# One matmul per tile for rows and gate logits, and one accumulation for places and counts, in a fused attention and expert kernel

## The chip, the cores and the metric

The kernel runs on one core of one Trainium2 chip. The time is the device time of one execution in microseconds (us). Before the change it is 1401.14 us, the median of 3 runs (1400.79 to 1401.62). The profile shown below is of one further execution, with a span of 1395.5 us. A core has five engines that run side by side, each with an instruction queue in order of its own: TensorE (PE, with its weight loads listed apart as PEld), VectorE (DVE), ScalarE (ACT), GpSimd (POOL) and SyncE (SP, which only issues transfers here). TensorE writes to PSUM; in this kernel ScalarE copies nearly all of it from there to SBUF.

## The reference

Two stages follow each other. The first is attention that keeps, for each query, only the 32 largest of its 576 scores:

```python
B, H, S, D = 8, 8, 576, 64
scores = q @ k.T / sqrt(D)                       # per batch and head
kth    = np.partition(scores, -32)[..., -32]     # the 32nd largest of each row
attn   = softmax(where(scores >= kth, scores, -1e9))
out    = attn @ v                                # (B, H, S, D)
```

The outputs of the heads are put side by side as rows of x, 4608 rows (tokens) of 512 numbers. The second stage sends each row through one of eight experts:

```python
logits = x @ w_gate                              # (4608, 512) @ (512, 8)
expert = argmax(logits); gate = softmax(logits)[expert]
y      = relu(x @ w1[expert]) @ w2[expert]       # 512 -> 1024 -> 512
out    = gate * y                                # in the order of the tokens
```

All numbers are 32-bit floats.

## The kernel before

**Units and groups.** Two heads make a unit, so a batch has four units (`n.u` is 0 to 3) and the kernel has 8 batches of four. The 576 queries of two heads are nine tiles of 128 rows. Two tiles make a group, so two units make nine groups and a batch has 18; the kernel has 144 groups. Each group goes through: scores on TensorE (line 269), copied to SBUF by ScalarE (line 276); the search for the 32nd largest on VectorE (lines 283 to 338); the mask and the exponential on ScalarE and GpSimd (lines 363, 372, 380); the transposes of the weights on TensorE (lines 391, 402, 404), copied by ScalarE (lines 395 to 412).

**The end of a unit.** When all tiles of a unit are done, `outputs` multiplies the transposed weights with the values (lines 424, 425) and ScalarE copies the result to `oT`, which holds the unit's outputs with the features on the partitions (128 partitions, two heads of 64) and the queries along the row. Then, tile by tile (KC = 5 tiles, the last a half):

- TensorE turns `oT` round by five transposes (lines 432 and 434), four into the PSUM bank `px` and one into the bank `pl`. These are rows of x.
- TensorE multiplies the same five tiles of `oT` with the gate's weights of this unit, `wg2`, 16 columns wide (8 experts for each of two heads; the other head's rows are zero) (line 437), also into `pl`.
- ScalarE copies the logits to `lt` (line 443), four tiles of rows to `x` (line 444) and the fifth (line 445).
- GpSimd divides both by the softmax sums: `logits` (lines 459 to 464) multiplies `lt` by the reciprocals `rz` and adds up `lg`, `rows` (line 470) multiplies the rows in place in `x`.

**The end of a batch.** `choice` (VectorE) finds each token's expert as a one-hot matrix `oh`. `ranks` (TensorE, lines 501 to 507) gives each token its place among the rows of its expert: how many tokens stand before it in its tile (a product with the triangle `before`), plus the tokens of the tiles ahead (products with `ones`), plus the running counts `run` (a product with the identity). A second chain in the same bank sums the new counts. `places` (VectorE, from line 517) reads the places, ScalarE copies the new counts to `run` (line 846), GpSimd scatters the rows to the experts' regions in HBM (line 538), and `table` (VectorE) lists the blocks of 128 rows that are full.

**The experts.** A full block is fetched, turned (line 655), multiplied with `w1` (line 680) and `w2` (line 695), scaled and scattered to the output (line 701). The products are cut into pieces, which are laid between the attention work of later batches.

**What sets the order.** The order of TensorE, ScalarE and VectorE is that of the program text, written by hand. `loop` walks over the 144 groups. A unit's end is a generator, `ending`, that goes on at named places in the groups after the unit's last: "products" (behind the scores of a later group), "relu" (on ScalarE ahead of the next copies of scores, line 276), "small", "rows" and so on. How many pieces of expert work go into which group is computed when the program is built, from a credit; it doesn't depend on the time that anything takes. Hence also fixed: what is left over for the end. All PSUM banks of the attention, `px`, `pl` and `rank` among them, are handed out in turn from a pool of two (`ps_t`, tag "t").

## Time and profile before

| stretch of the trace, us | what runs | busy share |
|---|---|---|
| 0 to 396 | attention of batches 0 to 2, almost no expert work | DVE 98%, PE 75% |
| 396 to 1112 | attention of batches 3 to 7 with expert work between | DVE 99%, PE 98% |
| 1112 to 1136 | last unit, last batch's choice and ranks | PE 91% |
| 1136 to 1380 | remaining expert blocks, 14.45 us each | PE 100%, DVE 2% |

The share of busy time over the whole run (PE 91%, DVE 79%) mixes these stages and says little; each is to be read by itself. The timeline lists every instruction with its start, its duration and the idle time of its engine ahead of it. Line 283 is the first VectorE instruction of each group's search, so the distance from one start of line 283 to the next is the time of a group. The sum over 18 groups gives the time of a batch:

| batch | 0 | 1 | 2 | 3 | 4 | 5 | 6 | 7 (17 groups) |
|---|---|---|---|---|---|---|---|---|
| time, us | 124.6 | 131.0 | 132.2 | 135.5 | 139.2 | 148.5 | 140.6 | 141.4 |
| PE busy in it, us | 91.2 | 98.9 | 104.8 | 133.1 | 136.3 | 146.8 | 137.9 | 139.7 |

In the first batches a plain group takes 7.02 us, with VectorE busy in all of it. From batch 3 on groups of 7.02 us stand beside groups of 8 to 9.7 us.

### The profile page before, as it was taken

How to read it: one execution, taken by the hardware profiler on the slowest of the kernel's cores; microseconds unless marked ns; L12 is line 12 of the kernel's file. 1: busy time of each engine (PE TensorE's matmuls, PEld its weight loads, DVE VectorE, ACT ScalarE, POOL GpSimd, SP SyncE). 2: the span in 40 equal slices, each digit the busy share in tenths (PEclk: the TensorE clock that was granted, in tenths of full speed). 3: DMA queues.
4: the chain of work that ended last, by engine and by line, in shares of the span. 5: the costliest groups of instructions: out<-in, count | busy, mean ns of one | idle time of the engine just before them, and what ended most of it. 6: DMA issues, size and time to landing. Idle time of an engine off the chain costs nothing. (4 is left out here: it accounts for less than half of the span.)

```text
span 1395.5 us, 24818 instructions
## 1 busy us (share of the span) xinstructions
PE 1267.8 (91%) x7778; PEld 872.2 (62%) x7778; DVE 1106.4 (79%) x4653; ACT 920.6 (66%) x2081; POOL 650.0 (47%) x804
## 2 busy tenths in 40 slices
PE   5777787677899999999999999999999999999995
PEld 3444454444567676767676666767676667677773
DVE  7999999999999999999999999999999920000000
ACT  4788878787888888787877787787777821111110
POOL 3455547455655665466555655565556521000000
PEclk8788878888899999999999999999999999999998
DMA  2000011001674266417553573357541859999890
GB/s 81 28 28 28 28 36 55 28 29 43 208 268 139 69 253 244 152 62 260 200 195 138 184 262 132 112 178 289 182 168 56 320 174 345 377 309 332 306 325 19
DMA packets 102222, 231.70 MB, mean 166 GB/s; under 512 B 5182, under 2 KB 25918, under 8 KB 102080
## 3 DMA queue, kind: packets, MB, share of 16 engines
q1 hardware_dynamic: 95328, 209.76, 42.9%
q0 software_dynamic: 6464, 19.97, 3.9%
q8 instruction: 63, 1.03, 0.3%
q14 instruction: 79, 0.65, 0.1%
q10 hardware_dynamic: 288, 0.30, 0.1%
HBM read 208.72 MB, written 22.33 MB: 166 GB/s over the span
## 5 line engine op out<-in xcount | busy, mean ns | idle before, releaser
L372 POOL TENSOR_TENSOR w<-s,w 128x576 f32<-128x576 f32 x288 | 407.6, 1435 | 464.0 <-ACT w L363 464.0
L680 PE MATMUL ph<-xTs,w 128*128 128x128 f32 x2560 | 311.7, 278 | 6.0 <-ACT xTs L657 6.0
L680 PEld LDWEIGHTS ph<-xTs,w 128*128 128x128 f32 x2560 | 301.4, 194 | 23.2 <-issue 14.9
L695 PE MATMUL py<-w,hT 128*128 128x512 f32 x640 | 292.9, 597 | 0.8 <-ACT hT L685 0.8
L331 DVE MAX8 tops<-scr 128x8 f32<-128x168 f32 x864 | 250.0, 323 | 0.1
L269 PE MATMUL sc<-qkb 64*128 64x288 f32 (+1 forms) x1280 | 224.0, 476 | 9.7 <-ACT s L276 5.2
L380 ACT ACTIVATE w<-w,nbias 128x576 f32<-128x576 f32 x288 | 224.7, 798 | 2.9 <-POOL w L372 2.8
L363 ACT ACTIVATE w<-s,low 128x576 f32<-128x576 f32 x288 | 207.6, 768 | 4.7
L391 PE MATMUL wTm<-ident,w 128*128 128x128 f32 x1152 | 173.7, 289 | 27.2 <-ACT x L444 17.8
L994 DVE CAST any_i<-pd 1x1 int32<-1x1 f32 x1 | 0.1, 146 | 237.6 <-PE pd L992 237.6
L695 PEld LDWEIGHTS py<-w,hT 128*128 128x128 f32 x640 | 114.5, 190 | 118.0 <-issue 115.6
L391 PEld LDWEIGHTS wTm<-ident,w 128*128 128x128 f32 x1152 | 139.1, 148 | 75.6 <-ACT x L444 19.0
L338 DVE MATCH_REPLACE8 scr<-tops,scr 128x168 f32<-128x168 f32 x576 | 178.9, 317 | 0.0
L276 ACT COPY s<-sc 128x576 f32<-128x576 f32 x288 | 170.5, 648 | 11.2 <-PE sc L269 11.1
L397 ACT COPY wT<-wTm 128x512 f32<-128x512 f32 x256 | 140.3, 609 | 41.4 <-PE wTm L391 41.2
L269 PEld LDWEIGHTS sc<-qkb 64*128 64x128 f32 (+1 forms) x1280 | 119.7, 198 | 74.1 <-issue 27.0
L424 PE MATMUL po<-wT,vb 128*64 128x288 f32 x1024 | 153.8, 448 | 0.4 <-ACT wTt L412 0.4
L701 POOL DMA_INDIRECT out_dram<-y,xg x40 | 41.7, 1043 | 216.4 <-ACT y L709 210.9
L322 DVE MAX8 few<-l 128x8 f32<-128x288 f32 x288 | 129.1, 448 | 0.0
L283 DVE TENSOR_TENSOR h<-s 128x576 f32<-128x576 f32 x144 | 115.9, 805 | 7.9 <-ACT s L276 7.9
L685 ACT ACTIVATE hT<-ph 128x512 f32<-128x512 f32 x80 | 48.9, 612 | 110.2 <-PE ph L680 110.2
L424 PEld LDWEIGHTS po<-wT,vb 128*64 128x64 f32 x1024 | 74.0, 150 | 76.2 <-issue 27.2
(127 smaller groups left out, 1524.4 us busy)
## 6 DMA issues: line engine op xcount, KB each, us to landing
w<-in_moe_w_dram SPq DMA_DIRECT2D x80, 2048.0 KB, 9.7
qkb<-in_qk_dram SPq DMA_DIRECT2D x31, 608.0 KB, 4.6
xg<-x_rows SPq DMA_DIRECT2D x40, 257.0 KB, 9.9
vb<-in_v_dram SPq DMA_DIRECT2D x32, 320.0 KB, 3.2
x_rows<-blank SPq DMA_DIRECT2D x5, 257.0 KB, 16.0
x_rows<-blank POOLq DMA_DIRECT2D x4, 257.0 KB, 9.0
x_rows<-x,posi POOLq DMA_INDIRECT x40, 3.1
out_dram<-y,xg POOLq DMA_INDIRECT x40, 6.2
```

The costliest lines, as they stand in the source:

```text
L269: nc.tensor.matmul(ps[rows, j, 0:HF], n.q[d, cols], n.k[d, keys], start=True, stop=True)
L276: lambda m=m, ps=ps: nc.scalar.copy(s[:, m, :, :], ps[:, :, 0:HF]) for m, ps in enumerate(got)
L331: nc.vector.max(out=tops[:, m, r * 8:(r + 1) * 8], in_=src[m])
L338: nc.vector.match_replace(out=scr[:, m, :], in_to_replace=tops[:, m, r * 8:(r + 1) * 8], in_values=src[m], imm_value=NEG,)
L363: nc.scalar.activation(w[:, m, :], s[:, m, :, :].rearrange("p j k -> p (j k)"), AF.Relu, scale=-STEEP, bias=low[:, m:m + 1],)
L372: k.last_pool = in_turn(nc.gpsimd.tensor_tensor(w[:, m, :], s[:, m, :, :].rearrange("p j k -> p (j k)"), w[:, m, :], op=ALU.subtract)).ins
L380: nc.scalar.activation(w[:, m, :], w[:, m, :], AF.Exp, scale=scale, bias=nbias[:, m:m + 1], accum_out=n.z[:, c:c + 1])
L391: nc.tensor.transpose(pm[:, c * P:(c + 1) * P], w[:, m, first:first + P], ident)
L397: nc.scalar.copy(wT[:, :, m, q], pm4)
L424: nc.tensor.matmul(po[r, 0:HF], n.v[:, c, r], wT[:, c, h, q], start=(c == 0), stop=False)
L680: nc.tensor.matmul(ph[:, f, :], n.w1[:, 0, dt, fc * P:(fc + 1) * P], n.xT[:, dt, :], start=(dt == 0), stop=(dt == DT - 1),)
L695: nc.tensor.matmul(py, hT[:, f, :], n.w2[:, 0, f, :], start=(f == 0), stop=(f == FT - 1))
```

## The change

For each tile of a unit's `oT`, the rows and the logits now come from one matmul: `oT` is loaded as the weights once, and the moving operand is a row of the new constant `turn`, in which the identity (128 columns) and the gate's weights of the unit (16 columns) stand side by side. The product is 144 columns wide. The five transposes and the separate gate products go away. Three tiles go to a first bank (432 columns), two to a second (288 columns), and ScalarE copies each bank with one instruction to a new tile `xl` in SBUF (one buffer), in place of the three copies to `lt` and `x`. GpSimd's instructions keep their number and shapes; `logits` reads and writes within `xl`, and `rows` now reads `xl` and writes `x`. For odd and even units the 16 columns stand on different sides of the identity, so that `turn` needs one identity for two units.

In `ranks`, the counts become a sixth tile of the places: one accumulation, 48 columns wide, started by the identity with `run` repeated six times. The second chain of products goes away.

The rest saves memory for that: the integer tiles of `iota_f` share one buffer, `slot_max` shrinks to two numbers that are repeated on reading, and two tiles of `table` get one buffer.

```diff
+    lw = 2 * E
+    turn = const.tile([P, U // 2, P + 2 * lw], F32, name="turn")
+    nc.vector.memset(turn, 0.0)
+    ident = turn[:, 0, lw:lw + P]
     make_identity(nc, ident)
+    for two in range(1, U // 2):
+        nc.gpsimd.tensor_copy(turn[:, two, lw:lw + P], ident)
...
-    for h in range(2):
-        r = slice(h * D, (h + 1) * D)
-        nc.vector.tensor_copy(wg2[r, :, h, :], wg[r, :, :])
+    for odd in range(2):
+        for h in range(2):
+            r = slice(h * D, (h + 1) * D)
+            at = odd * (lw + P) + h * E
+            nc.vector.tensor_copy(turn[r, :, at:at + E], wg[r, odd::2, :])
+
+    whole = const.tile([P, NSLOT], I32, name="whole")
...
-        i = const.tile(shape, I32, name=name + "_i")
+        i = whole[0:shape[0], 0:shape[1]]
...
-        px = bank("px")
-        for t in range(NC):
-            nc.tensor.transpose(px[:, t * P:(t + 1) * P], oT[:, starts[t]:starts[t] + P], ident)
-        pl = bank("pl")
-        nc.tensor.transpose(pl[:, 0:P], oT[:, starts[NC]:starts[NC] + P], ident)
-        lw = 2 * E
-        for t in range(KC):
-            nc.tensor.matmul(
-                pl[:, P + t * lw:P + (t + 1) * lw], oT[:, starts[t]:starts[t] + P],
-                wg2[:, n.u, :, :].rearrange("p h e -> p (h e)"), start=True, stop=True,
-            )
+        xw = P + lw
+        n.xl = k.small.tile([P, KC, xw], F32, name="xl", bufs=1)
+        put = []
+        for t0, t1 in ((0, KC - 2), (KC - 2, KC)):
+            px = bank("px")
+            for t in range(t0, t1):
+                nc.tensor.matmul(
+                    px[:, (t - t0) * xw:(t - t0 + 1) * xw], oT[:, starts[t]:starts[t] + P],
+                    turn[:, n.u // 2, odd * lw:odd * lw + xw], start=True, stop=True,
+                )
+            put.append((n.xl[:, t0:t1, :], px[:, 0:(t1 - t0) * xw].rearrange("p (t w) -> p t w", w=xw)))
         yield
-        n.lt = k.small.tile([P, KC, 2, E], F32, name="lt")
-        nc.scalar.copy(n.lt, pl[:, P:P + KC * lw].rearrange("p (t h e) -> p t h e", t=KC, h=2))
-        nc.scalar.copy(x[:, 0:NC, n.u * P:(n.u + 1) * P], px[:, :].rearrange("p (t d) -> p t d", t=NC))
-        nc.scalar.copy(x[:, NC, n.u * P:(n.u + 1) * P], pl[:, 0:P])
+        for to, px in put:
+            nc.scalar.copy(to, px)
...
-        in_turn(nc.gpsimd.tensor_tensor(xu, xu, _inner(rzb, D), op=ALU.mult))
+        xl = n.xl[:, :, at:at + P].rearrange("p t (h d) -> p t h d", h=2)
+        in_turn(nc.gpsimd.tensor_tensor(xu, xl, _inner(rzb, D), op=ALU.mult))
...
-        r.pos, r.run = rp[:, 0:KC * E], rp[:, 256:256 + E]
-        nc.tensor.matmul(r.pos, before, ohf, start=True, stop=False)
-        for i in range(1, KC):
-            nc.tensor.matmul(rp[:, i * E:KC * E], ones, ohf[:, 0:(KC - i) * E], start=False, stop=False)
-        nc.tensor.matmul(r.pos, ident, _ins(run[:, :], 1, KC), start=False, stop=True)
-        for i in range(KC):
-            nc.tensor.matmul(r.run, ones, r.oh[:, i, :], start=(i == 0), stop=False)
-        nc.tensor.matmul(r.run, ident, run, start=False, stop=True)
+        r.pos, r.run = rp[:, 0:KC * E], rp[:, KC * E:(KC + 1) * E]
+        nc.tensor.matmul(rp[:, 0:(KC + 1) * E], ident, _ins(run[:, :], 1, KC + 1), start=True, stop=False)
+        nc.tensor.matmul(r.pos, before, ohf, start=False, stop=False)
+        for i in range(1, KC + 1):
+            nc.tensor.matmul(
+                rp[:, i * E:(KC + 1) * E], ones, ohf[:, 0:(KC + 1 - i) * E], start=False, stop=(i == KC)
+            )
...
-        past = sm.tile([1, NSLOT, E], F32, name="past")
-        slot_f = sm.tile([1, 2, NSLOT], F32, name="slot_f")
+        past = sm.tile([1, NSLOT, E], F32, name="past", bufs=1)
+        slot_f = sm.tile([1, 2, NSLOT], F32, name="slot_f", bufs=1)
```

## The prediction, as it was put on record

> **What bounds the kernel now.** I read the slices of the page first, then a table of windows, then the timeline of the slow groups.

> ```profile
> PE   5777787677899999999999999999999999999995
> DVE  7999999999999999999999999999999920000000
> ...
> 150.00:300.00 150.00, 114.27 (x644) 72.13 (x645) 149.29 (x649) 119.38 (x277) 84.30 (x108) 0.84 0.13 41
> 600.00:750.00 150.00, 147.30 (x958) 102.04 (x956) 147.26 (x611) 117.19 (x269) 84.94 (x99) 1.00 0.54 193
> 1200.00:1300.00 100.00, 100.00 (x580) 73.22 (x579) 0.00 (x0) 16.43 (x28) 6.79 (x7) 1.00 0.93 328
> ```

> A window's columns are its length, then busy time of PE, PEld, DVE, ACT and POOL, the granted clock, and the DMA share. There are three regimes. Early, VectorE is the bound (149.29 of 150) and TensorE has room. At 600 to 750 both are near full: 147.30 and 147.26. At the end TensorE alone is the bound. The regime in the middle decides. Its batches are longer than batch 1 (131.0 us, with TensorE busy in 98.9 of it): by the table of batches, 4.5, 8.2, 17.5, 9.6 and, for 17 groups beside 124, some 17.4 us. That is 57 us over the VectorE bound, which TensorE's load causes, and a unit's end lies in such a place:

> ```profile
> 707.80 0.66 PE L432 MATMUL px<-ident,oT 128*128 128x128 f32 x4
> 708.30 0.27 PE L434 MATMUL pl<-ident,oT 128*128 128x128 f32 x1
> 708.41 1.19 PE L437 MATMUL pl<-wg,oT 128*128 128x16 f32 x10
> 709.44 2.82 PE L695 MATMUL py<-w,hT 128*128 128x512 f32 x6
> ...
> 704.81 1.44 ACT L363 ACTIVATE w<-s,low 128x576 f32<-128x576 f32 x2
> 709.63 0.23 ACT L443 COPY lt<-pl 128x80 f32<-128x80 f32 x1 [3.39 <-PE pl L437]
> 709.75 0.59 ACT L444 COPY x<-px 128x512 f32<-128x512 f32 x1
> 710.23 0.28 ACT L445 COPY x<-pl 128x128 f32<-128x128 f32 x1
> 710.39 1.21 ACT L276 COPY s<-sc 128x576 f32<-128x576 f32 x2
> ...
> 709.04 0.56 DVE L331 MAX8 tops<-scr 128x8 f32<-128x168 f32 x2
> 711.63 1.15 DVE L283 TENSOR_TENSOR h<-s 128x576 f32<-128x576 f32 x1 [2.04 <-ACT s L276]
> ```

> Columns: start, duration, instruction, idle time ahead and what ended it. ScalarE stands 3.39 us at the copy of `pl`, with the copies of scores queued behind it; VectorE then waits 2.04 us for those. The ranks do the same on a smaller scale:

> ```profile
> 586.55 0.41 PE L501 MATMUL rank<-oh,before 128*128 128x40 f32 x2
> ...
> 589.25 0.91 PE L680 MATMUL ph<-xTs,w 128*128 128x128 f32 x6
> ...
> 589.43 0.17 ACT L846 COPY run<-rank 128x8 f32<-128x8 f32 x1 [1.44 <-PE rank L507]
> ...
> 589.63 0.20 DVE L517 TENSOR_TENSOR pos<-rank,oh 128x40 f32<-128x40 f32 x1 [0.49 <-ACT run L846]
> ```

> [...] a 16-column gate product takes 1.03/10 = 0.103 us of the queue (708.41 to 709.44), little less than a 128-column expert product in the end phase (64 in 7.31 us, 0.114). [...] line 283 above lasts 1.15 us where its shortest are 0.73, beside GpSimd's line 470 (710.91 to 712.17). So a late ScalarE makes GpSimd late, and a late GpSimd can block VectorE at lines 291, 293 and 283. [...] the clock here is 0.84 in the early window and 1.00 later.

> **The rows and logits, on TensorE.** A multiplication of 32-bit floats is two passes (320 records of line 437 for 160 products), a transpose one. Removed per unit: five transposes and ten narrow passes, 1.64 us of the queue (707.80 to 709.44). Added: ten passes of 144 columns over 128 loaded ones, a shape that isn't in the trace. From the expert product, 0.114 x 144/128 = 0.128 us each; from line 695 (16 passes of 512 columns in 7.03 us), 0.124; from line 425 (288 columns, two in 0.59 us, 698.77 to 699.36), 0.147. I take 0.128, so 1.28 us, and keep 1.24 to 1.47. **Saved: 0.36 us per unit (0.17 to 0.40).**

> **On ScalarE.** Before, the score copies start 0.95 us after TensorE's last product (709.44 to 710.39). After, the first bank is full six passes in and its copy runs beside the last four passes: it starts near 707.80 + 0.77 + 0.19 = 708.76 (0.19 is the lag from 709.44 to 709.63) and holds ScalarE for 0.41 (512 columns held it 0.48). The second starts when TensorE ends, 709.08 + 0.19, and takes some 0.30 (288 columns at line 427, 699.56 to 699.86). The score copies start at about 709.57: 0.82 us sooner, of which 0.46 is ScalarE's. This is the value of a unit's end where ScalarE's queue holds VectorE up; 0.36 where only TensorE does. The next user of the first bank (line 391) also gets it sooner.

> **On GpSimd.** `logits` waits for both copies instead of the small one, from 709.57 + latency against 709.93: no later. Line 470 keeps its 1.26 us; if reading and writing apart ran at line 372's rate (1.39 us for 576 columns), it would take 1.55. I take 1.26. `xl` has one buffer: its next writer comes four groups after its reader, so that wait is over long before. Nothing.

> **The ranks.** Before 24 passes, 586.55 to 589.25 = 2.70 us. After 14: two for `run`, two for `before`, ten with `ones`. At 0.1125 (the eight of line 503 take 0.90) to 0.12 (line 501), about 1.60. **Saved: 1.1 us per batch**, for TensorE, for ScalarE at line 846 and for VectorE at line 517.

> **The constants.** VectorE clears 320 columns instead of 64 and copies the gate's weights four times instead of twice; it stands idle 3.93 us there for the gate's transfer. The shared `whole` chains iota and cast across two engines, three times. At worst VectorE meets that chain between its first folds, where it has 0.25 us of slack. 0 to 1 us; I take 0.3. The other memory edits are the same instructions: 0.

> **What of it reaches the end.** Batches 0 to 2: VectorE is the bound and hides it, but for one wait of 0.5 at the ranks (group 6 of batch 1). Ranks in batches 3 to 7: each falls in a group of 8.1 to 8.6 us with TensorE busy throughout, followed by one of 9.2 to 10.0, so all five count: 5.5. Unit ends: in batches 5 and 7 all four lie in or ahead of slow groups, one with the ScalarE wait: 0.82 + 3 x 0.36 = 1.9, twice 3.8. In batches 3, 4 and 6 three of four do (group 13 is 7.02 us, VectorE's own): 1.1 each, 3.2. Sum 13.0 us. Where a slow stretch ends, TensorE catches up and part of the gain is lost: I count three quarters, 9.8. From 1112 us on TensorE is the bound and everything counts: 0.36 + 1.1 = 1.5. Less 0.3 of the start: **11.0 us, 1390 us.**

> **Rivals.**
> 1. *Hidden anyway.* Both engines are near 98% in the middle. If VectorE is the bound there and its long instructions are its own, only its recorded waits can shrink: 5.4 us for scores and 2.1 for the ranks between 50 and 1090 us, of which about a third and all, so 3.9, less 1.2 for waits that reappear elsewhere, plus 1.5 at the end: 1397. Against it: the groups of 7.02 us beside those of 9.7.
> 2. *The lateness unwinds.* From 450 us on VectorE's two-input instructions lose some 40 us to blocking (what their durations in the timeline exceed each line's lower fifth by; line 291 lasts 0.44 us undisturbed, 0.545 in the mean and 1.5 at most), against 2.4 before 300 us. If a shorter ScalarE stall moves GpSimd out of their way, a third of that goes too: 11.0 + 13 = 24 us, 1377. Against it: most of the 144 line-372 pairs don't follow a unit's end.
> 3. *Slower.* The wide passes take 0.147 us, GpSimd's line 470 1.55, the start costs 1.0, and the shifted GpSimd work meets lines 291 and 293 in new groups: 20 units x 0.3 of line 470, of which half blocks, and six more blocks of 0.6: +3 + 3.6 + 1.0, less the ranks' 1.1 x 3: 1401.1 + 4.3 = 1405. Also, if TensorE has slack its clock may fall as in the early window. [...] Against: ScalarE gets earlier everywhere.

> **How the numbers follow.** Forecast (1385 to 1396) 0.55, rival 1 (1395 to 1400, a few of them within the bound) 0.20, rival 2 0.12, rival 3 0.13. The forecast's unknowns (pass 0.124 to 0.147, conversion a half to one) give 1386 to 1395. The range reaches into rivals 1 and 2: 1380 to 1400. Faster by over 0.2% (below 1398.3): 0.55 + 0.12 + 0.09 = 0.76. Within 0.2%: 0.11 of rival 1 and 0.01 of rival 3. Slower: 0.12.

> **What would show it.** The 144-column passes at about 0.128 us in the queue; ranks in 1.6 us; ScalarE's wait at the first copy of a unit's end (26.0 us in all now, at `lt`) falling by a third, VectorE's waits for scores by about as much; batches 3 to 7 shorter by 1.5 to 3 us each and batches 0 to 2 unchanged; the end phase 1.5 us shorter between the last search and the last product. I'm wrong if batches 3 to 7 keep their lengths (rival 1), if the blocked time at lines 283, 291, 293 changes by more than 5 us either way (rivals 2, 3), or if the 144-column pass is over 0.15 us.

## The result, and the profile after

The kernel after takes 1379.9 us (4 runs, 1379.57 to 1380.14) against 1401.12 (4 runs), 21.2 us less: a ratio of 0.9848, 95% interval 0.9831 to 0.9865. The two profiles differ by less, 1395.5 to 1378.2 us, since executions of the kernel before lie between 1395.4 and 1405.4 us over all rounds and the profiled one was a short one (1397.3). The stages of the two profiles:

| us | before | after | change |
|---|---|---|---|
| start to first search | 8.05 | 7.95 | -0.1 |
| batches 0, 1, 2 | 124.6, 131.0, 132.2 | 124.5, 131.7, 132.1 | +0.5 |
| batch 3 | 135.5 | 134.1 | -1.4 |
| batch 4 | 139.2 | 135.7 | -3.5 |
| batch 5 | 148.5 | 145.7 | -2.8 |
| batch 6 | 140.6 | 137.0 | -3.6 |
| batch 7 (17 groups) | 141.4 | 137.6 | -3.8 |
| last search to the last product | 279.3 | 276.7 | -2.6 |

The regimes are the same. First the slices of the page after, then two windows of it:

```profile
PE   5776777776799999999999999999999999999995
DVE  8999999999999999999999999999999820000000
```

```profile
600.00:750.00 150.00, 146.60 (x951) 102.23 (x949) 148.59 (x614) 118.15 (x266) 91.86 (x106) 1.00 0.55 194
1200.00:1300.00 100.00, 100.00 (x586) 73.80 (x585) 0.00 (x0) 16.50 (x28) 6.79 (x7) 1.00 0.90 321
```

In the middle window VectorE now works 148.59 of 150 us where it worked 147.26. The same unit's end as in the prediction, in the timeline of the kernel after (lines have moved by 7 to 9: 290 is the former 283, 450 is the copy of the banks, 479 the former 470):

```profile
702.76 1.49 PE L443 MATMUL px<-turn,oT 128*128 128x144 f32 x10
704.09 2.74 PE L703 MATMUL py<-w,hT 128*128 128x512 f32 x6
...
703.80 0.89 ACT L450 COPY xl<-px 128x432 f32<-128x432 f32 x2 [2.60 <-PE px L443]
704.58 1.19 ACT L283 COPY s<-sc 128x576 f32<-128x576 f32 x2
...
704.00 0.56 DVE L338 MAX8 tops<-scr 128x8 f32<-128x168 f32 x2
705.80 1.81 DVE L290 TENSOR_TENSOR h<-s 128x576 f32<-128x576 f32 x1 [1.24 <-ACT s L283]
```

Ten passes hold TensorE's queue for 1.33 us (702.76 to 704.09), 0.133 each, instead of 1.64. ScalarE's wait falls from 3.39 to 2.60, and its score copies start 0.49 us after TensorE's last pass instead of 0.95. VectorE waits 1.24 instead of 2.04, but then line 290 lasts 1.81: it stands beside GpSimd's line 479 (705.74 to 707.00). In the first profile of the kernel before, 50 of the 576 two-input instructions at lines 283, 285, 291 and 293 last over 0.1 us longer than their line's lower fifth, 1.2 us at most. All 50 are among the 143 that start while a TENSOR_TENSOR or TENSOR_SCALAR of GpSimd runs; this is what blocked means here. Of the 2016 MAX8 instructions at lines 322 and 331, 1167 start so, and none lasts 0.1 us longer. Over the run ScalarE's wait at the first copy is halved, from 26.0 us (the view of waits):

```profile
ACT xl L450 <- PE px L443: 13.4, 15, 2.6
```

VectorE's waits for scores between 50 and 1090 us fall from 5.4 to 2.5, those for the ranks from 2.1 to none. The ranks, in the timeline of the kernel after:

```profile
583.14 0.42 PE L510 MATMUL rank<-run,turn 128*128 128x48 f32 x2
...
583.61 1.26 PE L513 MATMUL rank<-oh,ones 128*128 128x40 f32 x10
...
584.72 2.92 PE L688 MATMUL ph<-xTs,w 128*128 128x128 f32 x24
...
584.90 0.17 ACT L854 COPY run<-rank 128x8 f32<-128x8 f32 x1 [0.32 <-PE rank L513]
```

They take 1.58 us (583.14 to 584.72) instead of 2.70.

### The profile page after: what moved, and what is told of

It is laid out like the page before. It is cut to its first block, busy times and chain, and to the rows that moved or that the text cites. A ratio compares the mean times of both kernels' runs of the same rounds, so it can differ in the third digit from the quotient of the medians.

```text
span 1378.2 us, 24231 instructions
## 1 busy us (share of the span) xinstructions
PE 1242.7 (90%) x7538; PEld 847.1 (61%) x7538; DVE 1097.6 (80%) x4655; ACT 919.9 (67%) x2049; POOL 649.9 (47%) x805
## 5 line engine op out<-in xcount | busy, mean ns | idle before, releaser
L688 PE MATMUL ph<-xTs,w 128*128 128x128 f32 x2560 | 307.6, 276 | 6.0 <-ACT xTs L665 6.0
L688 PEld LDWEIGHTS ph<-xTs,w 128*128 128x128 f32 x2560 | 298.3, 192 | 23.2 <-issue 14.9
L276 PE MATMUL sc<-qkb 64*128 64x288 f32 (+1 forms) x1280 | 224.1, 476 | 9.6 <-ACT s L283 5.2
L398 PE MATMUL wTm<-turn,w 128*128 128x128 f32 x1152 | 175.2, 291 | 34.5 <-ACT xl L450 21.1
L398 PEld LDWEIGHTS wTm<-turn,w 128*128 128x128 f32 x1152 | 140.2, 149 | 84.0 <-ACT xl L450 23.5
L283 ACT COPY s<-sc 128x576 f32<-128x576 f32 x288 | 169.9, 645 | 11.3 <-PE sc L276 10.7
L276 PEld LDWEIGHTS sc<-qkb 64*128 64x128 f32 (+1 forms) x1280 | 119.2, 197 | 73.2 <-issue 26.0
L290 DVE TENSOR_TENSOR h<-s 128x576 f32<-128x576 f32 x144 | 112.5, 781 | 4.4 <-ACT s L283 4.4
## 6 DMA issues: line engine op xcount, KB each, us to landing
x_rows<-blank SPq DMA_DIRECT2D x5, 257.0 KB, 13.8
```

Of the source, the lines that this page charges most:

```text
L276: nc.tensor.matmul(ps[rows, j, 0:HF], n.q[d, cols], n.k[d, keys], start=True, stop=True)
L283: lambda m=m, ps=ps: nc.scalar.copy(s[:, m, :, :], ps[:, :, 0:HF]) for m, ps in enumerate(got)
L398: nc.tensor.transpose(pm[:, c * P:(c + 1) * P], w[:, m, first:first + P], ident)
L688: nc.tensor.matmul(ph[:, f, :], n.w1[:, 0, dt, fc * P:(fc + 1) * P], n.xT[:, dt, :], start=(dt == 0), stop=(dt == DT - 1),)
```

## The experiments

The theories: **A**, TensorE's saved time counts once and in part, as in the prediction's sum. **B**, it counts about twice, because VectorE's blocked time goes with it. Others come in as the runs call for them. All changes below are against the kernel named; times are medians. The kernel before, timed again with each round, gave 1400.7 to 1401.2.

**1. The kernel before once more**, timed and profiled, unchanged.

> The kernel before, unchanged, timed and profiled once more. Its first profile spans 1395.5 us, 5.6 us under its timed median of 1401.1, while the kernel after has a span of 1378.2 and a median of 1379.9. Theory V (executions of the kernel before differ, and the profiled one was a short one): the span here is 1399 to 1400, some 2 us under the time, and the batches that are longer than in the first profile show where the 4 us lie. Theory P (a profiled execution of this kernel is really shorter): the span is again near 1395.5. Time: 1401 either way.

1400.8 us, 1396.7 to 1405.4, and a span of 1403.7: theory V in kind, though not its 1399 to 1400, since the profiled execution was itself the longest. Batches 2, 4, 5 and 7 are longer than in the first profile, by 1.6, 1.4, 1.7 and 3.4 us. Batch 2 lies in the early stage, where the clock changes often (in the first profile it goes to 0.5 24 times ahead of 396 us), and stays unexplained. In the other three a granted clock of 0.5 stands right behind the ranks, where the first profile has 1.00. The worst, in the windows and then the timeline of this run:

```profile
1022.00:1025.50 3.50, 3.50 (x31) 2.85 (x29) 3.50 (x13) 3.47 (x10) 0.48 (x1) 1.00 0.78 232
1025.50:1032.30 6.80, 6.80 (x14) 3.51 (x14) 6.01 (x31) 1.36 (x4) 2.63 (x4) 0.50 0.70 284
1032.30:1035.70 3.40, 3.40 (x10) 1.47 (x9) 3.40 (x22) 0.00 (x0) 0.00 (x0) 0.99 0.00 0
...
1024.71 1.52 PE L506 MATMUL rank<-oh,ones 128*128 128x8 f32 x10
1026.08 0.57 PE L507 MATMUL rank<-run,ident 128*128 128x8 f32 x2
1026.51 9.16 PE L695 MATMUL py<-w,hT 128*128 128x512 f32 x14
```

The column ahead of the DMA share is the clock. Fourteen expert passes take 9.16 us; the first profile of the same kernel has them in 6.25 at this place, and so has the kernel after. This was in no theory of mine. In this profile such windows follow four of the five ranks in the middle regime; in the first profile they follow one. In both they follow the last batch's ranks. By my estimate a window of 3.4 us at half the clock costs up to 1.7 us of TensorE's work (the 6.8 us above cost the fourteen passes 2.91), which is near the 1.4 and 1.7 us that batches 4 and 5, with one window each, got longer by.

**2 and 3. One half of the change at a time.** First the kernel before with the new `ranks`; then the kernel after with the old ones, whose edit begins and ends so:

```diff
-        nc.tensor.matmul(rp[:, 0:(KC + 1) * E], ident, _ins(run[:, :], 1, KC + 1), start=True, stop=False)
-        nc.tensor.matmul(r.pos, before, ohf, start=False, stop=False)
...
+        for i in range(KC):
+            nc.tensor.matmul(r.run, ones, r.oh[:, i, :], start=(i == 0), stop=False)
+        nc.tensor.matmul(r.run, ident, run, start=False, stop=True)
```

> The kernel before with the new ranks alone (14 passes for 24), rows and logits as before. Theory A (the recorded sum: TensorE's time counts once, three quarters of it in batches 3 to 7): 0.5 + 5.5 x 0.75 + 1.1 = 5.7 us less than before, 1395.4. Theory B (VectorE's blocked time goes with the lateness, so that each part gives about twice its sum): 9 to 12 us less, 1389 to 1392.

> The kernel after with the old ranks (24 passes), rows and logits by one product per tile. Theory A: 7.0 x 0.75 + 0.4 = 5.6 us less than before, 1395.5. Theory B: 9 to 12 us less, 1389 to 1392. If the parts don't add (one slow place cured by either), both this and the kernel with the ranks alone come near 1385.

Ranks alone 1391.2 (10.0 us less than the 1401.2 of before in these runs), rows alone 1391.9 (9.3 less). The halves add up, 19.3 of 21.2, and each gives far more than theory A's 5.7. Rows alone still has the old ranks, and the clock of 0.5 behind three of them; ranks alone has none. Windows of rows alone, then its timeline:

```profile
588.10:591.50 3.40, 3.40 (x18) 3.40 (x18) 3.31 (x22) 1.24 (x4) 2.12 (x4) 0.50 1.03 406
...
587.86 4.55 PE L689 MATMUL ph<-xTs,w 128*128 128x128 f32 x24
```

The same 24 passes behind the new ranks took 2.92 us above.

**4. A sixth product at each unit's end**, in the kernel after:

```diff
+            if t1 == KC:
+                nc.tensor.matmul(
+                    px[:, 2 * xw:3 * xw], oT[:, starts[NC]:starts[NC] + P],
+                    turn[:, n.u // 2, odd * lw:odd * lw + xw], start=True, stop=True,
+                )
```

> The kernel after with one product more at each unit's end: the fifth tile's 144 columns once more into the free columns of the second bank, which nothing reads. It gives TensorE 0.27 us back per unit, nearly all of what the new form saves there (1.64 to 1.33 us in the queue), and leaves ScalarE's two copies as they are. Theory A: 0.27 x 16 of the 32 units x 0.75 + 0.3 at the end = 3.5 us over the kernel after, 1383.4. Theory B: 6 to 9 us, 1386 to 1389. Theory S (what the rows bring comes from ScalarE's shorter queue and the banks): under 1.5 us, at most 1381.4.

1385.3, 5.4 us over the kernel after: neither A's 3.5 nor B's 6 to 9, and not S. Its cost in the queue, in the timeline:

```profile
706.69 0.41 PE L448 MATMUL px<-turn,oT 128*128 128x144 f32 x2
706.93 2.74 PE L708 MATMUL py<-w,hT 128*128 128x512 f32 x6
```

That is 0.24 us. For the 20 unit ends of batches 3 to 7 and the last at the end it makes 5.0 us. **In this kernel TensorE's time there counts at face value (a microsecond of its queue is a microsecond of the run), not at three quarters.**

**5. Ranks padded with wide passes**, in the kernel after:

```diff
+        for i in range(5):
+            nc.tensor.matmul(rp[:, 128:256], ones, ident, start=True, stop=True)
```

> The kernel after with ten passes more in the ranks (five products of ones with the identity, 128 columns wide, ahead of the accumulation, into columns that nothing reads). Near 1.15 us of TensorE more per batch, as much as the old ranks took over the new ones, but wide instead of 8 columns narrow. With the old, narrow ranks and the new rows the time was 1391.9, and the granted clock fell to 0.5 for 3.4 us right behind three of the ranks. Theory K (the narrow passes let the clock fall, and some 4 us of the 10 that the new ranks bring are that): no window of 0.5 behind any rank, and 1386 to 1387. Theory N (only the queue's time counts): 1390 to 1392, as with the old ranks.

1387.6, 7.7 us over the kernel after, 4.3 under the same kernel with the old ranks. The ranks hold the queue for 2.70 us, as before (584.41 to 587.11 in its timeline), and the clock stays:

```profile
587.10:590.50 3.40, 3.40 (x32) 3.40 (x32) 3.33 (x23) 1.85 (x4) 2.40 (x4) 1.00 1.04 412
...
584.41 1.38 PE L511 MATMUL rank<-turn,ones 128*128 128x128 f32 x10
...
587.11 2.92 PE L690 MATMUL ph<-xTs,w 128*128 128x128 f32 x24
```

Theory K, with its number missed by 0.6. The profiles of experiments 3 and 5 say where the 4.3 us lie: batches 4, 5 and 7, the three with a window of 0.5 in experiment 3, are shorter by 1.4, 1.7 and 1.7 us, and batches 3 and 6 agree within 0.1. The 1.12 us per batch cost 7.7 where the five ranks of the middle regime and the last make 6.7. In the profile batches 3 to 7 are longer by 5.7 for 5.6, face value. The end is longer by 2.6 for 1.1; a window of 0.5 stands there at 1116.3 us, ahead of the last ranks, which the kernel after hasn't.

**6. The same padding in the kernel before** (with the new ranks, rows as before).

> The kernel before with the new ranks and ten wide passes ahead of them: 24 passes and 2.7 us of TensorE's queue as in the kernel before, but ten of them 128 columns wide in place of narrow ones. Rows and logits as before. The same exchange gave 4.3 us in the kernel after (1391.9 to 1387.6). Theory K (narrow passes let the granted clock fall behind the ranks, in some executions): no window of 0.5 behind a rank in batches 2 to 6, 1396 to 1398, and runs within some 3 us of each other where those of the kernel before spread over 9. Theory N (only the queue's time counts): 1401, with the same spread.

1395.4 (1393.8 to 1397.5), 5.3 us under the kernel before, and no window of 0.5 behind a rank of batches 2 to 6 in its profile; time and spread (3.7) just miss theory K's numbers. Against the first profile of the kernel before, batches 3, 4, 5 and 7 agree within 0.1 us. Batch 6, with the one window of 0.5, is 1.4 us shorter. The windows behind its ranks, before and then in this run:

```profile
877.60:881.00 3.40, 3.40 (x18) 3.40 (x17) 3.39 (x22) 1.39 (x3) 1.73 (x4) 0.50 1.02 394
876.80:880.20 3.40, 3.40 (x33) 3.40 (x32) 3.40 (x22) 2.03 (x4) 1.99 (x4) 1.00 1.04 391
```

An equal number of passes in an equal time, ten of them wide instead of narrow, is worth 4 to 5 us in both kernels. Theory K. The padding by itself, new ranks with it (1395.4) against without (experiment 2, 1391.2), costs only 4.1 us for 6.7 here (4.4 for 5.6 in batches 3 to 7 of the two profiles), less than face value.

One rival would be luck in where the burst of ranks falls, for the clock changes on a grid of 3.41 us: in the profiles of the kernels before and after, the time from each change to the next is a whole multiple of 3.41 us (3.41 to 20.48 for the stretches at 0.5). Of the fifteen old ranks in batches 3 to 7 of three profiles, nine have 2.2 us or more of their 2.7 within one step of the grid, and eight of these are followed by 0.5. The other six have at most 2.0 us in one step, and none is. Of the ten padded ranks of experiments 5 and 6 four have over 2.5 us in one step, and none is followed by 0.5. So the place goes with which narrow bursts are hit, and it doesn't explain that no padded one was.

**7. One ScalarE copy more at each unit's end**, in the kernel after:

```diff
+        nc.scalar.copy(x[:, 0:3, n.u * P:(n.u + 1) * P], oT[:, 0:3 * P].rearrange("p (t d) -> p t d", t=3))
```

> The kernel after with one ScalarE copy more at each unit's end, behind the two copies of the banks and ahead of the next score copies: 384 columns of the unit's outputs from SBUF into x, where GpSimd overwrites them. It holds ScalarE some 0.37 us longer per unit; TensorE's work and the release of the banks are as in the kernel after. Theory S (ScalarE's shorter stay at the unit's end is a good part of the gain): 4 us or more over the kernel after, 1384 or more. Theory T (TensorE's queue is what counts, as the sixth product showed with 5.4 us for 0.27 us per unit): under 2 us, at most 1382.

1383.4, 3.5 us over the kernel after: between S and T. The copy holds ScalarE for 0.41 us in its timeline (706.32 to the score copies at 706.73). So ScalarE's time at these places counts too, at some 40% if taken over 21 unit ends (3.5 of 0.41 x 21 = 8.6). Its profile, taken in the shortest of its executions, has batches 3 to 7 longer by 1.7 us, some 20%.

**8. GpSimd's rows issued twice**, in the kernel after (the instruction of `rows` repeated).

> The kernel after with GpSimd's instruction that writes the rows (128 x 640, 1.26 us undisturbed) issued twice, which changes nothing in x. TensorE and ScalarE do the same. Theory G (GpSimd's own time blocks VectorE's two-input instructions, so the blocked time is a cost of its own): 5 us or more over the kernel after, 1385 or more. Theory T (VectorE is blocked where it would otherwise wait for TensorE's and ScalarE's late work, so the blocked time only shows the lateness): under 2 us, at most 1382.

1397.9, 18 us more, so theory G over the run. But the batches part: 0 to 6 are longer by 2.8, 3.5, 4.1, 2.6, 3.5, 0.0 and 1.0 us, and 7 by 0.0. (Up to 1.7 us of batch 4's 3.5 may be a window of 0.5 at 632.2 us, far from its ranks, behind 2.13 us in which TensorE waits for ScalarE.) Where VectorE is the bound the second instruction blocks it; a group of batch 2, GpSimd and then VectorE in the timeline of this run:

```profile
305.44 1.26 POOL L479 TENSOR_TENSOR x<-xl,rz 128x640 f32<-128x640 f32 x1
306.78 1.36 POOL L480 TENSOR_TENSOR x<-xl,rz 128x640 f32<-128x640 f32 x1
...
306.12 0.90 DVE L298 TENSOR_TENSOR few<-h 128x288 f32<-128x288 f32 x1
306.94 1.51 DVE L300 TENSOR_TENSOR hl<-h 128x288 f32<-128x288 f32 x1
```

Line 300 lasts 1.51 us; in the same group of the kernel after it lasts 0.45. Where TensorE is the bound (batches 5 and 7), 1.26 us more of GpSimd at four unit ends cost nothing: theory T holds there.

**9 to 12. The expert pieces spread more evenly**, in the kernel after. The factor by which a group's share of pieces is multiplied, by the group's tile; in the second by group, in proportion to TensorE's room:

```diff
-                share = {0: 0.5, 1: 1.2, 2: 1.6, 3: 0.5, 2 * NC: 1.4}[tile]
+                share = {0: 0.9, 1: 1.0, 2: 1.2, 3: 0.9, 2 * NC: 1.0}[tile]
```

> The kernel after with the expert pieces spread more evenly over the groups: the factors by tile 0.8, 1.1, 1.3, 0.9 and 0.9 for the shared tail, instead of 0.5, 1.2, 1.6, 0.5, 1.4. The work is the same. In batches 3, 4 and 6 groups of 8 to 9 us stand beside groups of 7.02, so there is room. Theory L (local overload of TensorE is the cost): 3 to 10 us less than the kernel after, 1370 to 1377. If the lateness only moves to other groups: 1376 to 1384.

> The kernel after with factors for each of the nine groups of a pair of units, in proportion to what TensorE has left beside the attention work there: 7.0 us less 2.2 for scores and transposes, less 1.4 for a half of the outputs (groups 0, 3, 4, 8), less 1.3 for the new rows (groups 1, 5), less 0.9 for the tails' scores (group 0). Theory L: more than with factors by tile, 5 to 12 us less than the kernel after, 1368 to 1375. If lateness only moves: 1376 to 1384.

> The kernel after with the expert pieces spread by tile with the factors 0.9, 1.0, 1.2, 0.9 and 1.0 for the tail, flatter than the 0.8, 1.1, 1.3, 0.9, 0.9 that gave 1374.2. If flat is what helps: 1368 to 1374. If the place of single pieces decides: 1374 to 1382.

> The same with 0.8, 1.1, 1.3, 0.7 and 1.1, less on the unit's last tile and more on the tail than the one that gave 1374.2. If the last tile's group, where the outputs begin, is the crowded one: 1370 to 1374. If the place of single pieces decides: 1374 to 1382.

1374.2, 1378.1, **1369.6** (the factors in the diff) and 1371.0. The third has a ratio of 0.9784 to the kernel before (0.9759 to 0.9809), the fastest of all. Its batches 3 to 7 take 132.7, 132.8, 143.0, 134.9 and 135.8 us: 3 and 4 are near the 131 of VectorE's bound. In batches 3 to 7 its groups of over 8 us are 20 of 89, where the kernel after has 29, and behind the last search 1402 expert passes are left in both kernels, so no work was moved into or out of the end. Spreading TensorE's load without making it smaller gives 10.3 us more, half as much again as the change itself. The computed proportions (1378.1) were worse than the guesses by tile, so the room per group that I reckoned is not the right measure.

## Why the prediction was wrong

It said 1390 and a range of 1380 to 1400; the time was 1379.9. The direction and the places were right, the sum was half of the gain. **The step that failed most is the price of the ranks:** it is their queue time alone, and the clock of the work behind them stands at nothing. The runs show 4.3 to 5.3 us there, beside 4.1 to 7.7 for their queue time. **The second is what reaches the end:** 9.8 us in batches 3 to 7, where 13.8 arrived with the clock set apart. By its steps:

- **What bounds it: right.** Batches 0 to 2 hide the change (+0.5 us in all), batches 3 to 7 and the end carry it.
- **Sizes on TensorE: right.** 0.133 us per wide pass for 0.128, so 0.31 saved per unit for 0.36; ranks 1.58 us for 1.60.
- **Size on ScalarE: right, its place wrong.** The score copies start 0.46 us sooner, as worked out. I counted that only at the two places with a recorded wait of VectorE. By experiment 7 the 0.46 is worth some 2 us (by the profile) to 4 us (by the median) and not one.
- **GpSimd and the constants: right.** Line 479 takes 1.26 us at the end shown; the first search starts 0.1 us sooner, where I took 0.3 later.
- **"I count three quarters": too little here.** From the kernel of experiment 6 to the kernel after, neither with a window of 0.5 in batches 3 to 7, these batches get 13.8 us shorter. The prediction's sum was 13.0 ahead of the cut by a quarter, 9.8 behind it. But no one factor holds: experiments 4 and 5 give 5.4 for 5.0 and 7.7 for 6.7 in the kernel after, and the padding 4.1 for 6.7 in the kernel before. Why the two kernels differ stays open.
- **The ranks' narrowness: missed.** I costed the ranks by their queue time alone, and put the clock into rival 3, with the wrong sign: I feared slack would lower it. It fell to 0.5 behind 24 narrow passes (eight of fifteen bursts), and wide passes for ten of them give 4.3 to 5.3 us (experiments 5 and 6).
- **The end phase: only half explained.** It lost 2.6 us instead of 1.5. The kernel before has a clock of 0.5 for 3.4 us from 1137.0 on, behind its last ranks. But experiment 6 has none there and one at 1108.9 and takes 279.4 us, and experiment 3 has none at all in that phase and takes 278.7, so the last ranks' clock isn't shown to be the cause.

Summed up from the runs: the clock behind the ranks 5.3 (experiment 6), and from there to the kernel after 15.5 (1395.4 to 1379.9), 20.8 for 21.2 measured. In the profiles the 15.5 are 13.8 in batches 3 to 7 and 2.7 at the end, less 1.0 in batches 0 to 2. TensorE's saved queue time makes 11.8 of the 13.8 (0.31 x 20 and 1.12 x 5), and the 2.0 left are of the size that experiment 7's profile gives for ScalarE. That is a sum that fits, not a proof of each term.

**Rival 2** came nearest in time (1377), but its reason isn't shown. In batches 3 to 7 VectorE's blocked time (durations of its two-input instructions above each line's lower fifth) did fall from 41.8 to 30.9 us, and with the sixth product it rose again by 5.1, as these batches got longer by 4.7. But experiment 8 says that blocked time is a cost of its own only where VectorE is the bound, and in batches 5 and 7 takes the place of a wait. How much of the 10.9 us is cause and how much only shows TensorE's lateness stays open for batches 3, 4 and 6.

My own test for being wrong, a change of blocked time by over 5 us at lines 283, 291 and 293, was just not met: 34.6 us over the run became 29.7. Nor were the other two (batches 3 to 7 that keep their lengths, a pass of over 0.15 us). What I had missed, the clock behind the ranks, had no sign among them.

## What to carry to other kernels

Where two engines are both near full, look at the length of each repeated group: groups at the floor beside groups well above it are a sign that work is badly spread. Here its time in the crowded groups counted between 0.6 of face value and a little over it, and spreading it better gave half as much again as the change. Don't cost narrow matrix products by their columns (here a pass of 16 took 0.103 us of the queue and one of 128 took 0.114), and cost them also by what may happen to the clock of the work behind them (the same 24 passes took 4.55 us with a window of 0.5 and 2.92 at 1.00): look at the granted clock in the few us after a burst. Profile a kernel twice before building a difference of 1% on one trace.

## What the runs showed of the hardware that I had not expected

That the few moving columns bring the 0.5 about is my reading of the exchange for wide passes, worth 4.3 us in the kernel after and 5.3 in the kernel before; by what rule the clock is granted was not shown.
